# A list scheduler with new costs, a model of VectorE and GpSimd on SBUF, and a new table of priorities

## The chip, the cores and the metric

The kernel runs on one core of one Trainium2 chip. The metric is the device time of one execution in microseconds (us). The kernel before took 1358.99 us (median of three runs, 1357.96 to 1361.76).

In the text PE is the matmul engine (TensorE), DVE is VectorE, ACT is ScalarE, POOL is GpSimd and SP is the engine that issues most transfers.

## The reference, cut to what matters

```
attention, 8 batches x 8 heads, 576 positions x 64; k and v averaged over groups of 8 positions
    -> softmax(q k' / 8) v          = x, 4608 tokens x 512
dense   h = x @ w_in (512 x 2048);  g = h * sigmoid(h);  x = g @ w_out
experts skip = x @ w_skip > 0;  logits = x @ w_gate (8 experts)
    every token with skip > 0 goes to its best expert e:
    x += gate * (relu(x @ w1[e]) @ w2[e])
```

All is float32. Each dense product is split into a high and a low part, so that three matmuls in a faster format (fp32r) replace one.

## The kernel before, in words

There are two stages. The **dense stage** (`dense`, L450) does attention, the dense layer and the routing. Tokens are cut into 36 tiles of 128 and 18 chunks of two tiles (numbers 0 to 17). The **expert stage** (`experts`, L1028) follows in fixed order; its first products (`xm1p`, L952) need the weights of the first expert, split into high and low parts, and gathered tokens.

The dense stage is not written in order. `op(...)` enters each step with its costs per engine, the steps it comes after and the buffers it takes; `schedule` (L649) then issues them one at a time. Among the steps that could start earliest it takes the one with the largest `height`: the length of the longest chain behind it, into which a `bonus` per kind and phase is added (`bonus_of`, L452). Where a step may run on several engines, the one with the lowest end time plus `EXTRA` is taken. Engines then run their own lists strictly in order, each step waiting for its semaphores. The steps that matter below, with their lines:

- `w` (L153) loads 512 KB of a weight; there are 32 such pieces. `abs` L162, `low` L166, `hi` L180 on ACT, `mix` L170 and `or` L175 on DVE turn it into a high part; `lo` (L184, DVE or POOL) makes the low part.
- `vsum` (L221) and `kput` (L201, L205, L207) average v and k. `sc` L260, `mx` L265, `ex` L274, `ns` L279, `nr` L285, `pt` L290, `pc` L231 and `pv` L302 are the attention of one tile; `xh` and `xl` (L318) split its result.
- For each chunk j and each of 16 blocks f: `mm1` (12 matmuls, L324 to L326), `th` L331 on ACT, `sw` L337 on DVE, `gh` L341 on ACT, `gl` (L346, DVE or POOL), `mm2` (6 matmuls, L356 to L358). `mm1` of block f needs the pieces 2f, `mm2` the pieces 2f+1.
- `ev` L365 takes a finished tile out, `st` L371 stores it, 18 `dot` per chunk (L376) give its logits, `ra` (L389 to L397), `rp` (PE, L404), `re` (ACT, L409), `rg`, `rb` (L429 to L437) and `rs` (POOL, L440, two per chunk) place its tokens in the lists of the experts.
- At the end of the dense stage: `ft` (L789 to L805) finds the largest expert from the lists of the chunks up to 15, `fi` (L874) reads its first indices, `l1` and `l2` (L889) load its weights, `ga` (L923) gathers tokens, `xp` (L934) and `xq`/`xr` turn them, `s1h` (L905), `s1l` (L909) split w1, `s2h`, `s2l` split w2. `ft` comes after `rb` of chunk 15, `fi` after `rs` of chunk 15, `l2` and `ti` (L808) after `ra` of chunk 16.

Of the kernel before, what the change touches and what calls it, by code (L numbers as in the profile page):

```python
# [18 lines left out]
B, H, S, D = 8, 8, 576, 64  # L19
# [33 lines left out]
def body(tc, const, q, k, v, w_in, w_out, w_skip, w_gate, w_r, w1, w2, out, x2d, lst, base, nch, nxt):  # L53
# [3 lines left out]
    with ExitStack() as ctx:  # L57
# [94 lines left out]
        def load_w(h):  # L152
            nc.sync.dma_start(out=stage(h), in_=(w_out if h % 2 else w_in)[h // 2])  # L153
# [296 lines left out]
        def dense():  # L450
            ops, last, st = {}, {}, {}
            bonus_of = {  # L452
# [8 lines left out]
            }  # L461
# [13 lines left out]
            def op(name, cost, fn, after=(), take=None, bonus=0.0, linger=0.0):  # L475
                linger += 0.9 * ("S" in cost)
                bonus += bonus_of.get(name[0], {}).get(phase(*name), 0.0)
                ops[name] = (cost, fn, [a for a in after if a], take, bonus, linger)
# [4 lines left out]
            for h in range(2 * NF):  # L483
                op(("w", h), {"S": 1.46}, lambda e, h=h: load_w(h), [h > 3 and ("or", h - 4)])
                last["cx", h] = [("hi", h), ("lo", h)]
                op(("abs", h), {"A": 0.52}, lambda e, h=h: conv_abs(h), [("w", h), h > 0 and ("abs", h - 1)],
                   ("x2", ("cx", h)))
                op(("low", h), {"A": 0.61}, lambda e, h=h: conv_low(h), [("w", h)])
                op(("mix", h), {"V": 0.6}, lambda e, h=h: conv_mix(h), [("abs", h), ("low", h)])
                op(("or", h), {"V": 0.6}, lambda e, h=h: conv_or(h), [("mix", h)])  # L490
                op(("hi", h), {"A": 0.52}, lambda e, h=h: conv_hi(h), [("or", h)])
                op(("lo", h), {"G": 1.23, "V": 0.6}, lambda e, h=h: conv_lo(e, h), [("hi", h)],
                   bonus=-35.6 * h)
# [5 lines left out]
            ways = {0: ["T", "V", "V", "G"], 1: ["VG", "G", "VG", "V"]}  # L499
            price = {"V": 1.34, "G": 2.01}  # L500
            for b in range((tiles * 128 - 1) // S + 1):
                old = b > 1 and ((b - 1) * S - 1) // 128
                for hp in range(HP):
                    s = spot.get(("k", hp)) if b == 0 else None
                    free = [b == 1 and ("clear",), b > 1 and ("sc", old, hp // 2)]
                    last["k", b, hp] = [("kput", b, hp)]
                    op(("k", b, hp), {"S": 0.82}, lambda e, b=b, hp=hp, s=s: put_in((b, hp), k_load(b, hp, s)),
                       [b > 0 and (("k", b, hp - 1) if hp else ("v", b - 1, POOL - 1))], None if s else ("kv", ("k", b, hp)))
# [33 lines left out]
            for i in range(tiles):  # L542
# [3 lines left out]
                last["q", i] = [("sc", i, 1)]  # L546
                op(("q", i), {"S": 0.73}, lambda e, i=i: load_q(i), [i > 0 and ("q", i - 1)], ("q", ("q", i)))
                for g in range(2):
# [23 lines left out]
            for j in range(nch):  # L572
                for f in range(NF):
                    n = slot.get((j, f), -1)

                    def back(name, k):
                        return n - k in at and (name, *at[n - k])

                    last["h", j, f], last["t", j, f], last["g", j, f] = [("sw", j, f)], [("gl", j, f)], [("mm2", j, f)]
                    op(("mm1", j, f), {"T": 1.31}, lambda e, j=j, f=f: put_in(("h", j, f), mm1(j, f)),  # L580
                       [("xl", TPC * j + t) for t in range(TPC)]
# [8 lines left out]
                       [("gh", j, f)], ("gl", ("g", j, f)))  # L590
                    op(("mm2", j, f), {"T": 1.29}, lambda e, j=j, f=f: mm2(j, f),
                       [("gl", j, f), ("lo", 2 * f + 1), f > 0 and ("mm2", j, f - 1), back("mm1", -1)]
# [3 lines left out]
                for t in range(TPC):  # L596
                    i = TPC * j + t
                    dots = [("dot", i, c) for c in range(E + 1)] if j < nch - 1 else []
                    last["x2", i] = dots + [("st", j, t)]
                    op(("ev", j, t), {"A": 0.48, "V": 0.6}, lambda e, j=j, t=t: evac(e, j, t),  # L600
                       [("mm2", j, NF - 1), t > 0 and ("ev", j, t - 1), j > 1 and ("rs", j - 2, TPC - 1), ("or", 2 * NF - 1)],
                       ("x2", ("x2", i)))
                    op(("st", j, t), {"S": 1.46}, lambda e, i=i: store(i), [("ev", j, t)])
                    for c in range(E + 1):
                        if j < nch - 1:
                            op(("dot", i, c), {"V": 0.72}, lambda e, i=i, c=c: dot(i, c), [("ev", j, t), ("router",)])
# [12 lines left out]
            op(("setup",), {"G": 1.5}, lambda e: setup2(), [("lo", 3)])  # L619
            op(("blank",), {"S": 1.0}, lambda e: blank_lists(), [("setup",)])  # L620
            op(("router",), {"S": 8.0}, lambda e: load_router(), [("or", h) for h in range(2 * NF - 4, 2 * NF)])
            ops[("ra", 0)][2].append(("setup",))

            if nxt:
                z, free = nch - 1, ("xl", tiles - 1)
                op(("ft",), {"V": 1.6}, lambda e: first_table(), [free, ("rb", z - 2)])
                ops[("rp", z - 1)][2].append(("ft",))
                op(("fi",), {"S": 0.3}, lambda e: first_idx(), [("ft",)] + [("rs", z - 2, t) for t in range(TPC)])
                op(("l1",), {"S": 6.0}, lambda e: load_1(), [("fi",)])
                op(("l2",), {"S": 6.0}, lambda e: load_2(), [("ra", z - 1), ("l1",)])  # L630
                op(("ga",), {"G": 2.1}, lambda e: gather(0), [("fi",)] + [("st", j, t) for j in range(z) for t in range(TPC)],
# [17 lines left out]
        def schedule(ops, last):  # L649
            unit = {"T": nc.tensor, "A": nc.scalar, "V": nc.vector, "G": nc.gpsimd, "S": nc.sync}  # L650
            room_for = dict(a=2, h=2, o=2 * TPC, x2=4, t=2, gh=3, gl=3, tr=2, kv=3, q=2)
            EXTRA = {"V": 2.34, "G": 0.0, "A": 1.5}
            SIGNAL, SAME, ISSUE, COLD = 0.135, 0.13, 1.75, 30.0

            def gap(a, b):
                if a == b:
                    return SAME * (a != "T")
                return {"T": 0.46, "S": ISSUE}.get(b, SIGNAL + 0.06 * ("T" in a + b or "G" in a + b))

# [13 lines left out]

            held, end, free = {r: [] for r in room_for}, {}, {u: ISSUE * (u == "S") for u in unit}
            known = {}

            def earliest(n):
                if n not in known:
                    known[n] = {}
                    for u in ops[n][0]:  # L680
                        known[n][u] = max([end[d][0] + gap(end[d][1], u)
                                           + ops[d][5] for d in ops[n][2]], default=0.0)
                cost, _, _, take, _, _ = ops[n]
                wait = []
# [539 lines left out]
```

## Time and profile before

| | us |
|---|---|
| median of three runs | 1358.99 |
| the profiled execution | 1359.34 |
| its span, first to last instruction | 1357.6 |
| PE busy | 1279.5 (94%) |
| DVE busy | 817.3 (60%) |
| POOL busy | 642.3 (47%) |
| ACT busy | 567.3 (42%) |

Matmuls are pipelined, so the busy time of PE is no measure of its best speed. The granted TensorE clock has two levels, 1.2 and 2.4 GHz; a window with 0.91 was partly at the lower one. The engine shares are means over stages: the weight pieces are converted in the first 136 us, the dense stage ends at 1005 us, and the expert stage takes the rest.

### The profile page before, as it was taken

How to read it: one execution, taken by the hardware profiler on the slowest of the kernel's cores; microseconds unless marked ns; L12 is line 12 of the kernel's file. 1: busy time of each engine (PE TensorE's matmuls, PEld its weight loads, DVE VectorE, ACT ScalarE, POOL GpSimd, SP SyncE). 2: the span in 40 equal slices, each digit the busy share in tenths (PEclk: the TensorE clock that was granted, in tenths of full speed). 3: DMA queues.
4: the chain of work that ended last, by engine and by line, in shares of the span. 5: the costliest groups of instructions: out<-in, count | busy, mean ns of one | idle time of the engine just before them, and what ended most of it. 6: DMA issues, size and time to landing. Idle time of an engine off the chain costs nothing. (4 is left out here: it accounts for less than half of the span.)

```text
span 1357.6 us, 24535 instructions
## 1 busy us (share of the span) xinstructions
PE 1279.5 (94%) x8508; PEld 1133.2 (83%) x8508; DVE 817.3 (60%) x1963; ACT 567.3 (42%) x1619; POOL 642.3 (47%) x692
## 2 busy tenths in 40 slices
PE   5778999999999999999999999999899999999895
PEld 3557989898888888889888988988789999989674
DVE  7898295276374584574674673759954232333785
ACT  5767443444444334444444443434332121223573
POOL 6889445543653554265366333333652212133664
PEclk9989999999999999999999999999999999999998
DMA  8554131111121121012011110110401111427761
GB/s 244 182 190 169 69 107 31 56 48 40 57 66 43 30 87 48 9 62 79 25 61 41 37 40 12 45 63 1 171 32 48 56 41 56 164 72 257 237 240 36
DMA packets 51311, 113.84 MB, mean 84 GB/s; under 512 B 12311, under 2 KB 13335, under 8 KB 51024
## 3 DMA queue, kind: packets, MB, share of 16 engines
q1 hardware_dynamic: 44960, 96.39, 21.9%
q0 software_dynamic: 6192, 15.49, 3.5%
q8 instruction: 80, 1.31, 0.4%
q14 instruction: 79, 0.65, 0.2%
HBM read 134.58 MB, written 26.62 MB: 119 GB/s over the span
## 5 line engine op out<-in xcount | busy, mean ns | idle before, releaser
L346 POOL TENSOR_TENSOR gl<-t,gh 128x256 fp32r<-128x256 f32 x287 | 234.8, 820 | 314.2 <-ACT gh L341 224.0
L324 PE MATMUL psh<-xh,w_hi 128*128 128x256 f32 x1152 | 334.3, 290 | 12.2 <-DVE t L337 9.8
L326 PE MATMUL psh<-xh,w_lo 128*128 128x256 f32 x1152 | 324.8, 282 | 5.7 <-POOL w_lo L184 5.7
L325 PE MATMUL psh<-xl,w_hi 128*128 128x256 f32 x1152 | 324.7, 282 | 3.0 <-DVE xl L318 3.0
L376 DVE SCALAR_TENSOR_TENSOR junk<-x,wb 128x512 bf16<-128x512 f32 x306 | 268.8, 878 | 14.7 <-ACT x L365 8.5
L324 PEld LDWEIGHTS psh<-xh,w_hi 128*128 128x128 f32 x1152 | 219.0, 190 | 30.3 <-DVE t L337 13.9
L337 DVE SCALAR_TENSOR_TENSOR t<-t,psh 128x256 f32<-128x256 f32 x288 | 119.1, 415 | 206.5 <-ACT t L331 205.5
L356 PE MATMUL pso<-v_hi,gh 128*128 128x512 f32 x576 | 236.1, 410 | 0.8 <-ACT gh L341 0.8
L358 PE MATMUL pso<-v_hi,gl 128*128 128x512 f32 x576 | 227.2, 394 | 6.7 <-POOL gl L346 6.7
L357 PE MATMUL pso<-v_lo,gh 128*128 128x512 f32 x576 | 227.8, 395 | 0.0
L325 PEld LDWEIGHTS psh<-xl,w_hi 128*128 128x128 f32 x1152 | 219.1, 190 | 10.1 <-DVE xl L318 3.2
L326 PEld LDWEIGHTS psh<-xh,w_lo 128*128 128x128 f32 x1152 | 218.8, 190 | 6.5 <-POOL w_lo L184 6.5
L341 ACT CAST gh<-t 128x256 fp32r<-128x256 f32 x288 | 116.9, 407 | 219.3 <-DVE t L337 204.0
L331 ACT ACTIVATE t<-psh 128x256 f32<-128x256 f32 x288 | 110.5, 384 | 211.2 <-PE psh L326 177.7
L358 PEld LDWEIGHTS pso<-v_hi,gl 128*128 128x128 f32 x576 | 109.0, 189 | 37.3 <-POOL gl L346 11.7
L356 PEld LDWEIGHTS pso<-v_hi,gh 128*128 128x128 f32 x576 | 109.1, 189 | 14.9 <-ACT gh L341 1.0
L357 PEld LDWEIGHTS pso<-v_lo,gh 128*128 128x128 f32 x576 | 109.5, 190 | 12.9
L1005 POOL DMA_INDIRECT out_dram<-own,room x27 | 28.2, 1044 | 173.6 <-DVE own L1003 120.3
L961 ACT ACTIVATE v_hi<-p 128x256 fp32r<-128x256 f32 x88 | 33.5, 383 | 183.4 <-PE p L960 175.2
L274 ACT ACTIVATE room<-pss,mx 128x72 f32<-128x72 f32 x288 | 88.3, 319 | 51.6 <-DVE mx L266 48.7
L962 DVE SCALAR_TENSOR_TENSOR v_hi<-p,v_hi 128x256 fp32r<-128x256 f32 x88 | 37.0, 424 | 114.8 <-ACT v_hi L961 102.6
L958 PE MATMUL p<-xh,w_hi 128*128 128x256 f32 x352 | 101.1, 287 | 0.1
(190 smaller groups left out, 2318.2 us busy)
## 6 DMA issues: line engine op xcount, KB each, us to landing
more<-in_w_dram SPq DMA_DIRECT2D x72, 512.0 KB
room<-in_w_dram SPq DMA_DIRECT2D x40, 512.0 KB
wb<-in_w_dram SPq DMA_DIRECT2D x36, 512.0 KB
room<-in_k_dram SPq DMA_DIRECT2D x32, 288.0 KB
room<-in_q_dram SPq DMA_DIRECT2D x36, 256.0 KB
room<-in_v_dram SPq DMA_DIRECT2D x64, 144.0 KB
out_dram<-x SPq DMA_DIRECT2D x36, 256.0 KB
x2d<-x SPq DMA_DIRECT2D x36, 256.0 KB
```

Source lines behind the costliest of these rows:

```text
L324: nc.tensor.matmul(out=ps, lhsT=w4_hi[:, f, kk], rhs=xh[:, kk], start=(kk == 0), stop=False)
L325: nc.tensor.matmul(out=ps, lhsT=w4_hi[:, f, kk], rhs=xl[:, kk], start=False, stop=False)
L326: nc.tensor.matmul(out=ps, lhsT=w4_lo[:, f, kk], rhs=xh[:, kk], start=False, stop=(kk == KD - 1))
L331: nc.scalar.activation(out=t, in_=ps, func=ACTF.Tanh, scale=0.5)
L337: nc.vector.scalar_tensor_tensor(out=t, in0=t, scalar=1.0, in1=ps, op0=ALU.add, op1=ALU.mult)
L341: nc.scalar.copy(out=gh, in_=t)
L346: eng.tensor_tensor(out=gl, in0=t, in1=gh.bitcast(F32), op=ALU.subtract)
L356: nc.tensor.matmul(out=ps, lhsT=gh[:, ts], rhs=v_hi[:, f], start=(f == 0), stop=False)
L357: nc.tensor.matmul(out=ps, lhsT=gh[:, ts], rhs=v_lo[:, f], start=False, stop=False)
L358: nc.tensor.matmul(out=ps, lhsT=gl[:, ts], rhs=v_hi[:, f], start=False, stop=(f == NF - 1))
L376: nc.vector.scalar_tensor_tensor(out=junk, in0=x2_t[i], scalar=1.0, in1=wb[:, e * DM:e * DM + DM], op0=ALU.mult, op1=ALU.mult, accum_out=l ...
L958: nc.tensor.matmul(out=ps, lhsT=W1h4[:, kk, m], rhs=xh[:, kk], start=(kk == 0), stop=False)
```

## The change: new costs, contention and priorities for the scheduler

No instruction's work changes; the steps are the same 3313. New are their costs (`w` and `st` 1.46 to 1.95, `pv`, `mm1`, `mm2` and others), the terms by which an engine is chosen, and the table `bonus_of`, which now has nearly every kind. Transfers go through one modelled queue. A step of DVE in `SHARED` waits in the model for POOL's recent steps, and a step of POOL for DVE's.

```
-                "rb": {0: 40, 1: 120, 3: -216, 8: 160}, "rs": {0: -30, 1: -30, 2: 15, 3: -2},
+                "rb": {0: 42.4, 1: 166.4, 2: -22.6, 3: -214.7, 8: -125.3},
+                "rs": {0: -23.3, 1: -15.7, 2: 19.8, 3: -9.6},
...
+                "dot": {0: 21.8, 1: 111.7, 2: -15.4, 3: 263.4, 8: -143.5}, "w": {0: -236.8},
...
-                linger += 0.9 * ("S" in cost)
...
-                op(("w", h), {"S": 1.46}, lambda e, h=h: load_w(h), [h > 3 and ("or", h - 4)])
+                op(("w", h), {"S": 1.95}, lambda e, h=h: load_w(h), [h > 3 and ("or", h - 4)])
...
-                op(("l1",), {"S": 6.0}, lambda e: load_1(), [("fi",)])
+                op(("l1",), {"S": 8.0}, lambda e: load_1(), [("fi",)])
...
-            EXTRA = {"V": 2.34, "G": 0.0, "A": 1.5}
-            SIGNAL, SAME, ISSUE, COLD = 0.135, 0.13, 1.75, 30.0
+            SHARED, APART = ("ns", "mix", "or", "lo", "nr", "vsum", "vput", "gl", "dot", "kput"), ("rs", "ga", "setup", "ti")
+            FIRST = {"V": 0.786439, "G": 0, "A": 0.394171}
+            LATER = {"V": 1.58663, "G": 0, "A": -0.769199}
+            FILL, HOLD, KEEP = 181.563, 0.9, 0.6
+            SIGNAL, SAME, ISSUE, REACH, COLD, IDLE, WARM = 0.135, 0.05, 0.45, 2.0, 1.8, 3.4, 4.0
...
-                    t = max(free[u], known[n][u])
+                    t, more = max(free[u], known[n][u]), 0.0
...
-                    if u == "T" and t < COLD:
-                        c = 2 * c
-                    rank = t + c + (EXTRA[u] if len(cost) > 1 else 0.0)
-                    if best is None or rank < best[0]:
-                        best = (rank, t, t + c, u)
+                    if u == "S":
+                        return t, t, max(queue[0], t + REACH) + c, u
+                    if u == "T" and (t - quiet[0] > IDLE or ran[0] < WARM):
+                        c = COLD * c
+                    elif u == "V" and n[0] in SHARED:
+                        for a, b in wide["G"][-4:]:
+                            if a <= t + 0.05 and b > t:
+                                t = max(t, a + (b - a) * HOLD)
+                    elif u == "G":
+                        for a, b in wide["V"][-4:]:
+                            if a <= t < b:
+                                t = b
+                        if len(cost) > 1 and t < FILL:
+                            more = KEEP * c
+                    if len(cost) > 1:
+                        more += (LATER if t > FILL else FIRST).get(u, 0.0)
+                    if best is None or t + c + more < best[0]:
+                        best = (t + c + more, t, t + c, u)
...
+                elif u == "G" and n[0] not in APART or u == "V" and n[0] in SHARED:
+                    wide[u].append((t, t1))
```

By count of instructions DVE now has 30 of the 32 `lo` (3 before), 16 of the 56 `vsum` and `vput` (1 before) and 10 of the 288 `gl` (1 before); POOL has the rest, and all 72 `nr` (69 before). The lines from L491 on stand 18 to 39 lines lower in the new file.

**PE, start of the dense layer.** The first `mm1` of chunk 1 (its input is `xh_484` before, `xh_457` after) and what stands ahead of it. Before:

```order
L356 MATMUL pso_496<-v_hi_103,gh_806 128x512
L357 MATMUL pso_496<-v_lo_110,gh_806 128x512
L358 MATMUL pso_496<-v_hi_103,gl_827 128x512
L260 MATMUL pss_865<-room_106 64x144 x4
L324 MATMUL psh_875<-xh_484,w_hi_101 128x256
L325 MATMUL psh_875<-xl_485,w_hi_101 128x256
```

After:

```order
L356 MATMUL pso_491<-v_hi_103,gh_564 128x512
L357 MATMUL pso_491<-v_lo_110,gh_564 128x512
L358 MATMUL pso_491<-v_hi_103,gl_568 128x512
L324 MATMUL psh_596<-xh_457,w_hi_101 128x256
L325 MATMUL psh_596<-xl_458,w_hi_101 128x256
```

Before, ten `mm1` and nine `mm2` of chunk 0 stand ahead of it; after, four of each. From there on the blocks of the two chunks alternate.

**PE, end of the dense stage.** The three last `rp` (L404, L405: `psr`), of chunks 15, 14 and 16. Before, the first two stand among the blocks of chunk 16:

```order
L358 MATMUL pso_10501<-v_hi_103,gl_10962 128x512
L404 LDWEIGHTS triu_94
L404 MATMUL psr_11014<-ohb_10951,triu_94 128x16
L405 LDWEIGHTS ones_95
L405 MATMUL psr_11014<-ohb_10951,ones_95 128x16
L404 LDWEIGHTS triu_94
L404 MATMUL psr_11017<-ohb_10983,triu_94 128x16
L405 LDWEIGHTS ones_95
L405 MATMUL psr_11017<-ohb_10983,ones_95 128x16
L324 MATMUL psh_11022<-xh_10133,w_hi_101 128x256
```

After, all three stand behind the last `mm2` of chunk 17 (`pso_11140`), and the expert stage's `xp` and first product follow:

```order
L358 MATMUL pso_11140<-v_hi_103,gl_11470 128x512
L404 LDWEIGHTS triu_94
L404 MATMUL psr_11484<-ohb_10825,triu_94 128x16
L405 LDWEIGHTS ones_95
L405 MATMUL psr_11484<-ohb_10825,ones_95 128x16
L404 LDWEIGHTS triu_94
L404 MATMUL psr_11487<-ohb_11023,triu_94 128x16
L405 LDWEIGHTS ones_95
L405 MATMUL psr_11487<-ohb_11023,ones_95 128x16
L404 LDWEIGHTS triu_94
L404 MATMUL psr_11636<-ohb_11614,triu_94 128x16
```

What hangs on `rp` of chunks 14 and 15 (`rb`, `ft`, `fi`, `l1`, `ga`) has moved behind the last matmul of the stage with it.

**ACT, end of the dense stage.** The splits of the first expert's w1 (`s1h`: `w_hi<-room`, L905 before, L944 after). Before:

```order
L341 CAST gh<-t 128x256
L905 CAST w_hi<-room 128x1024
L331 ACTIVATE t<-psh 128x256
L905 CAST w_hi<-room 128x1024
L341 CAST gh<-t 128x256
L905 CAST w_hi<-room 128x1024
L331 ACTIVATE t<-psh 128x256
L409 ACTIVATE lg<-lg 128x2x8
L905 CAST w_hi<-room 128x1024
L341 CAST gh<-t 128x256
```

After, behind the last `gh`:

```order
L341 CAST gh<-t 128x256
L365 ACTIVATE x_11537<-pso 128x512
L365 ACTIVATE x_11539<-pso 128x512
L365 ACTIVATE x_11561<-pso 128x512
L365 ACTIVATE x_11570<-pso 128x512
L409 ACTIVATE lg<-lg 128x2x8
L944 CAST w_hi<-room 128x1024 x4
L979 CAST xh<-pst 128x4x128 x2
L944 CAST w_hi<-wb 128x1024 x3
```

The splits stood between the blocks of chunk 17; now they stand behind `re` of chunk 16 (L409), which waits for the 18 `dot` of that chunk. On DVE these 18 `dot` follow `ft`, which follows the last `sw`; on SP `l1` follows the stores of chunk 17.

## Rows read from the trace of the kernel before

**Rows 1.** Windows: engine busy us (instructions), granted clock, DMA share, GB/s.
```profile
core 0: us, PE busy (x) PEld busy (x) DVE busy (x) ACT busy (x) POOL busy (x), PEclk, DMA share, GB/s
40.00:140.00 100.00, 79.22 (x463) 66.66 (x462) 85.44 (x98) 66.14 (x157) 86.18 (x85) 0.91 0.54 180
140.00:180.00 40.00, 40.00 (x308) 35.79 (x306) 17.45 (x41) 20.51 (x67) 20.94 (x23) 1.00 0.24 72
180.00:955.00 775.00, 768.31 (x5363) 684.66 (x5360) 481.33 (x1447) 322.43 (x1075) 357.45 (x442) 1.00 0.14 45
955.00:1006.00 51.00, 46.89 (x286) 41.26 (x285) 39.03 (x89) 20.41 (x43) 32.59 (x29) 0.97 0.33 114
```
**Rows 2.** Timeline of PE: first matmuls of chunks 0 and 1 (start, us, instruction).
```profile
41.36 0.59 PE L324 MATMUL psh<-xh,w_hi 128*128 128x256 f32 x1
...
96.09 0.39 PE L324 MATMUL psh<-xh,w_hi 128*128 128x256 f32 x1
```
**Rows 3.** Lines, 0 to 135 us: count, busy us, mean ns, idle ahead.
```profile
L170 DVE SCALAR_TENSOR_TENSOR cx<-cx,wb 128x512 int32<-128x512 int32 x32 | 41.8, 1307 | 5.6 <-ACT wb L166 3.3 <-POOL room L205 1.3 <-issue 1.0
L175 DVE SCALAR_TENSOR_TENSOR cx<-wb,cx 128x512 int32<-128x512 int32 x32 | 38.0, 1189 | 0.6
...
L184 POOL TENSOR_TENSOR w_lo<-cx,w_hi 128x512 fp32r<-128x512 f32 x15 | 23.8, 1587 | 4.7 <-ACT w_hi L180 4.4
L184 POOL TENSOR_TENSOR v_lo<-cx,v_hi 128x512 fp32r<-128x512 f32 x14 | 22.0, 1571 | 1.5 <-ACT v_hi L180 1.4
L221 POOL TENSOR_TENSOR room<-room 72x512 f32<-72x512 f32 x13 | 19.2, 1480 | 5.7 <-DMA room<-in_v_dram 5.7
```
**Rows 4.** Timeline of DVE, 38 to 53 us.
```profile
38.46 0.66 DVE L184 TENSOR_TENSOR w_lo<-cx,w_hi 128x512 fp32r<-128x512 f32 x1
...
47.35 3.73 DVE L170 SCALAR_TENSOR_TENSOR cx<-cx,wb 128x512 int32<-128x512 int32 x1
...
52.48 0.68 DVE L175 SCALAR_TENSOR_TENSOR cx<-wb,cx 128x512 int32<-128x512 int32 x1
```
**Rows 5.** Timeline of POOL in the same stretch, and its last conversion.
```profile
48.54 0.74 POOL L346 TENSOR_TENSOR gl<-t,gh 128x256 fp32r<-128x256 f32 x1
49.24 1.30 POOL L184 TENSOR_TENSOR w_lo<-cx,w_hi 128x512 fp32r<-128x512 f32 x1
...
134.49 1.30 POOL L184 TENSOR_TENSOR v_lo<-cx,v_hi 128x512 fp32r<-128x512 f32 x1
```
**Rows 6.** Waits of PE, 960 to 1060 us: us in total, times, longest.
```profile
PE psh L324 <- DVE t L337: 4.1, 2, 2.1
```
**Rows 7.** Timeline of DVE, 945 to 968 us.
```profile
945.51 0.16 DVE L389 TENSOR_REDUCE rmx<-lg 128x2 f32<-128x16 f32 x1
...
946.82 0.17 DVE L397 CAST ohb<-oh 128x16 bf16<-128x16 f32 x1
...
949.55 0.16 DVE L429 TENSOR_TENSOR ds<-psr,base 128x8 f32<-128x8 f32 x1
...
950.91 0.16 DVE L437 TENSOR_TENSOR du<-dd,cm 128x2 int32<-128x2 f32 x1
...
954.09 0.15 DVE L794 SCALAR_TENSOR_TENSOR room<-base,room 1x8 f32<-1x8 f32 x1
...
955.90 0.15 DVE L805 TENSOR_TENSOR room<-room 1x8 f32<-1x8 f32 x1
...
967.04 0.69 DVE L376 SCALAR_TENSOR_TENSOR junk<-x,wb 128x512 bf16<-128x512 f32 x1
...
967.76 0.69 DVE L376 SCALAR_TENSOR_TENSOR junk<-x,wb 128x512 bf16<-128x512 f32 x1
```
**Rows 8.** Timeline of POOL, 992 to 1021 us.
```profile
992.90 2.40 POOL L909 TENSOR_TENSOR w_lo<-wb,w_hi 128x1024 fp32r<-128x1024 f32 x1 [0.20 <-ACT w_hi L905]
...
1017.70 1.00 POOL L440 DMA_INDIRECT lst<-row,du  x1 [3.09 <-DVE du L437]
1020.11 0.97 POOL L440 DMA_INDIRECT lst<-row,du  x1 [1.41 <-DMA lst<-row,du]
```
**Rows 9.** Timeline of SP's issues, 964 to 968 us.
```profile
964.81 0.41 SPq L874 DMA_DIRECT2D room<-lst  x1
965.42 2.10 SPq L889 DMA_DIRECT2D room<-in_w_dram  x4
```
**Rows 10.** Timeline of ACT, 993 us: two splits in a row.
```profile
993.45 1.99 ACT L905 CAST w_hi<-wb 128x1024 fp32r<-128x1024 f32 x2
```
**Rows 11.** Timeline of PE, 1015 to 1017 us.
```profile
1015.89 0.28 PE L958 MATMUL p<-xh,w_hi 128*128 128x256 f32 x1
1016.01 0.29 PE L959 MATMUL p<-xl,w_hi 128*128 128x256 f32 x1
...
1016.31 0.41 PE L958 MATMUL p<-xh,w_hi 128*128 128x256 f32 x1
1016.52 0.41 PE L959 MATMUL p<-xl,w_hi 128*128 128x256 f32 x1
```

More of the change, by code (lines that the diff above doesn't have):

```diff
@@ L499, in dense @@
             ways = {0: ["T", "V", "V", "G"], 1: ["VG", "G", "VG", "V"]}
-            price = {"V": 1.34, "G": 2.01}
+            price = {"V": 1.34, "G": 2.4}
             for b in range((tiles * 128 - 1) // S + 1):
@@ L506, in dense @@
                     last["k", b, hp] = [("kput", b, hp)]
[L507 removed]
+                    op(("k", b, hp), {"S": 1.1}, lambda e, b=b, hp=hp, s=s: put_in((b, hp), k_load(b, hp, s)),
                        [b > 0 and (("k", b, hp - 1) if hp else ("v", b - 1, POOL - 1))], None if s else ("kv", ("k", b, hp)))
@@ L546, in dense @@
                 last["q", i] = [("sc", i, 1)]
-                op(("q", i), {"S": 0.73}, lambda e, i=i: load_q(i), [i > 0 and ("q", i - 1)], ("q", ("q", i)))
+                op(("q", i), {"S": 0.98}, lambda e, i=i: load_q(i), [i > 0 and ("q", i - 1)], ("q", ("q", i)))
                 for g in range(2):
@@ L562, in dense @@
                 last["pv", i] = [("xl", i)]
-                op(("pv", i), {"T": 0.8 + 0.24 * len(bs)}, lambda e, i=i, p=pool_f, t=tag: pv_all(i, p, t),
+                op(("pv", i), {"T": 0.95 + 0.35 * len(bs)}, lambda e, i=i, p=pool_f, t=tag: pv_all(i, p, t),
                    [("pc", i, 1), j > 1 and ("mm1", j - 2, NF - 1)]
@@ L579, in dense @@
                     last["h", j, f], last["t", j, f], last["g", j, f] = [("sw", j, f)], [("gl", j, f)], [("mm2", j, f)]
-                    op(("mm1", j, f), {"T": 1.31}, lambda e, j=j, f=f: put_in(("h", j, f), mm1(j, f)),
+                    op(("mm1", j, f), {"T": 1.42}, lambda e, j=j, f=f: put_in(("h", j, f), mm1(j, f)),
                        [("xl", TPC * j + t) for t in range(TPC)]
@@ L590, in dense @@
                        [("gh", j, f)], ("gl", ("g", j, f)))
-                    op(("mm2", j, f), {"T": 1.29}, lambda e, j=j, f=f: mm2(j, f),
+                    op(("mm2", j, f), {"T": 1.39}, lambda e, j=j, f=f: mm2(j, f),
                        [("gl", j, f), ("lo", 2 * f + 1), f > 0 and ("mm2", j, f - 1), back("mm1", -1)]
@@ L602, in dense @@
                        ("x2", ("x2", i)))
-                    op(("st", j, t), {"S": 1.46}, lambda e, i=i: store(i), [("ev", j, t)])
+                    op(("st", j, t), {"S": 1.95}, lambda e, i=i: store(i), [("ev", j, t)])
                     for c in range(E + 1):
@@ L619, in dense @@
             op(("setup",), {"G": 1.5}, lambda e: setup2(), [("lo", 3)])
-            op(("blank",), {"S": 1.0}, lambda e: blank_lists(), [("setup",)])
-            op(("router",), {"S": 8.0}, lambda e: load_router(), [("or", h) for h in range(2 * NF - 4, 2 * NF)])
+            op(("blank",), {"S": 1.15}, lambda e: blank_lists(), [("setup",)])
+            op(("router",), {"S": 9.2}, lambda e: load_router(), [("or", h) for h in range(2 * NF - 4, 2 * NF)])
             ops[("ra", 0)][2].append(("setup",))
@@ L627, in dense @@
                 ops[("rp", z - 1)][2].append(("ft",))
-                op(("fi",), {"S": 0.3}, lambda e: first_idx(), [("ft",)] + [("rs", z - 2, t) for t in range(TPC)])
-                op(("l1",), {"S": 6.0}, lambda e: load_1(), [("fi",)])
-                op(("l2",), {"S": 6.0}, lambda e: load_2(), [("ra", z - 1), ("l1",)])
+                op(("fi",), {"S": 0.2}, lambda e: first_idx(), [("ft",)] + [("rs", z - 2, t) for t in range(TPC)])
+                op(("l1",), {"S": 8.0}, lambda e: load_1(), [("fi",)])
+                op(("l2",), {"S": 8.0}, lambda e: load_2(), [("ra", z - 1), ("l1",)])
                 op(("ga",), {"G": 2.1}, lambda e: gather(0), [("fi",)] + [("st", j, t) for j in range(z) for t in range(TPC)],
@@ L657, in gap @@
                     return SAME * (a != "T")
-                return {"T": 0.46, "S": ISSUE}.get(b, SIGNAL + 0.06 * ("T" in a + b or "G" in a + b))
+                return {"T": 0.43, "S": 0.2}.get(b, SIGNAL + 0.06 * ("T" in a + b or "G" in a + b))
             users, left = {n: [] for n in ops}, {n: len(o[2]) for n, o in ops.items()}
@@ L672, in schedule @@
                 height[n] = min(ops[n][0].values()) + ops[n][4] + max((SIGNAL + height[u] for u in users[n]), default=0)
-            held, end, free = {r: [] for r in room_for}, {}, {u: ISSUE * (u == "S") for u in unit}
-            known = {}
+            held, end, free = {r: [] for r in room_for}, {}, {u: 0.0 for u in unit}
+            known, wide = {}, {"V": [], "G": []}
+            queue, ran, quiet = [0.0], [0.0], [-9.0]
             def earliest(n):
+                cost, _, deps, take, _, _ = ops[n]
                 if n not in known:
[L679 to L683, printed above, removed]
+                    known[n] = {u: max([end[d][0] + gap(end[d][1], u) + ops[d][5] for d in deps], default=0.0)
+                                for u in cost}
                 wait = []
@@ L706, in schedule @@
                 t0 = min(e[1] for e, _ in can)
-                (_, _, t1, u), n = max((c for c in can if c[0][1] <= t0), key=lambda c: height[c[1]])
+                (_, t, t1, u), n = max((c for c in can if c[0][1] <= t0), key=lambda c: height[c[1]])
                 take = ops[n][3]
@@ L712, in schedule @@
                 end[n], free[u] = (t1, u), t1
+                if u == "T":
+                    ran[0], quiet[0] = t1 - t if t - quiet[0] > IDLE else ran[0] + t1 - t, t1
+                elif u == "S":
+                    queue[0], free[u] = t1, t + ISSUE
+                elif u == "G" and n[0] not in APART or u == "V" and n[0] in SHARED:
+                    wide[u].append((t, t1))
                 ready.remove(n)
```

2 lines of the change are left out of this document (1 added, 1 removed), and 31 rows, old and new, of the table bonus_of.

## The prediction, made before the changed kernel ran

> **What bounds the kernel now.** I read the page's shares first (the table above), then the windows by stage, then for each window with idle PE the timelines of the engines that PE waits for. PE is busy for 94% of the span, so only its idle time and its time at the lower clock can be won. [rows 1] show where that lies. From 40 to 140 us PE is busy for 79.22 of 100 us and the granted clock is 0.91; from 140 to 180 it is never idle; from 180 to 955 it is idle for 6.7 us of 775; from 955 to 1006 for 4.1 of 51, at 0.97. So there are two places to look at: the fill, in which the weights are converted, and the end of the dense stage. Between them nothing is to be had and little should be lost.
>
> In the fill the idle time is 100 - 79.22 = 20.8 us. A mean of 0.91 over two levels, of which the lower is half, means that the clock was low for 18% of the window, 18 us; PE did work for some 79% of that, at half speed, so about 7 us are lost to the clock. Together about 28 us. At the end of the dense stage it is 4.1 us and, by the same reckoning (6% of 51 us, halved), 1.5.
>
> Why is PE idle in the fill? In that window DVE is busy for 85.4% and POOL for 86.2% [rows 1]; a block of a chunk can only start when two more pieces are converted. [rows 5] show the last conversion at 134.49. Chunk 1, whose input needs two more tiles of attention, starts at 96.09, 55 us after chunk 0 at 41.36 [rows 2]. Until then each pair of pieces releases one block for PE only: 12 matmuls of 256 columns at 0.12 us [rows 11] and 6 of 512, for which I take twice that: 1.4 + 1.4 = 2.8 us.
>
> **Term 1: the fill.** The change puts chunk 1 behind four blocks of chunk 0 in place of ten (the first of the orders above) and then alternates. From the fifth block on each pair of pieces releases 5.6 us of work, and conversions arrive every 95 / 16 = 5.9 us (41 to 136 us): PE is then nearly full and its clock should stay up. What is not won is the stretch before the fifth block: about 5 us of the 28 lie in its first 16 to 20 us. Of the remaining 23 I leave 3 for the difference of 5.6 and 5.9 and for ACT (66% busy). **20 us are won.** The bounds: 8, if conversions end some 12 us later than they do now, since the blocks that are last in both chunks wait for the last pieces; 33, if the whole 28 goes and chunk 0 also starts 5 us earlier.
>
> Do the conversions keep their pace? DVE takes 27 more `lo`, 0.66 us each when alone [rows 4], 18 us, and 15 averaging sums, for which the nearest row is the same one and POOL's 1.48 [rows 3] the other end: 10 to 22 us, I take 12. POOL loses 27 x 1.58 = 43 us and 15 x 1.48 = 22 us [rows 3]. DVE may get time back too: its `mix` and `or` last 1.307 and 1.189 us on the mean [rows 3], where a single one without company takes 0.68 [rows 4]; 32 x (1.307 + 1.189 - 2 x 0.68) = 36 us of stretching. So DVE's gain of 36 pays for its new 30, and the conversions should end where they do, near 136 us.
>
> The stretch is no rounding: one `mix` started at 47.35 and took 3.73 us, while POOL ran a `gl` of 0.74 at 48.54 and a `lo` of 1.30 at 49.24 [rows 4, 5]. The Trainium skill, page "SBUF — State Buffer", section "Who interferes with whom", states that a DVE instruction with two inputs in SBUF and a POOL instruction that reads SBUF shut each other out for a whole instruction. The row agrees: the `mix` ended about when POOL's two were over. By that rule the two engines' sum counts for the conversions (an estimate: 45 us of DVE and 84 of POOL before, 84 and 48 after, for the kinds that meet), and it stays the same: they would not end sooner, the fill would win by the order of PE alone, and the third rival below would have little to stand on. By the row alone DVE could gain up to the 36 us and end sooner.
>
> **Term 2: the end of the dense stage.** Here the orders show a loss. `rp` of chunks 14 and 15 stood between blocks of chunk 16; now they stand behind the last `mm2` of chunk 17. What depends on them ran under the matmuls of chunks 16 and 17 (`rb` of chunk 15 or 14 at 949.55, `ft` at 954.09, `fi` at 964.81, `l1` at 965.42 [rows 7, 9]); after the change nothing of PE is left to hide it. Let t = 0 be the end of that last `mm2`. The chain in the new order:
>
> - `rp` 15 and 14 and their signals, estimated at 0.6 us. Two `rb`, 949.55 to 951.07 = 1.52 us each [rows 7]: 3.6.
> - `ft`, 954.09 to 956.05 = 1.96 [rows 7]: 5.6. It stands ahead of 18 `dot` of chunk 16 on DVE, 0.72 apart [rows 7]: 18.6. `ra` of chunk 16, 945.51 to 946.99 = 1.48 [rows 7]: 20.0; `re` on ACT, some 0.3: 20.3.
> - ACT has its `s1h` behind that `re`: four at 1.0 [rows 10]: 24.3. In the meantime DVE does `rg` and `rb` of chunk 16 (1.5 and 1.5: 23.5), and POOL has its `rs` ahead of its two `s1l`: 1.0 [rows 8], 24.5.
> - `s1l` on POOL, 2.40 each [rows 8]: 26.9 and 29.3; DVE has two of these in between (twice 0.66 for twice the width [rows 4]), and one of them in POOL's way makes it 30.5.
> - The expert stage's first product needs all quarters of w1, so PE stands until about 30.5 but for its transposes, and then starts at the lower clock: 0.21 us a matmul in place of 0.12 [rows 11], 1.5 us in the first sixteen.
>
> Beside it runs the load: two `rs` per chunk for 14 and 15, 2.41 apart [rows 8], 3.6 + 4 x 2.41 = 13.2 without overlap; `fi`, then `st` of chunk 17, then four issues of `l1` in 2.10 [rows 9]: issued at about 15.5, landed by some 22 us. That is 1 to 2 us earlier than the splits can use it, and so costs nothing; it would be next if the `dot` were quicker.
>
> So PE waits about 30.5 us and loses 1.5 to the clock: 32. What goes is the wait of before: 4.1 us of PE for DVE's `t` [rows 6], in which the `dot` were in the way, and the 1.5 of clock: 5.6. On POOL the splits of w2 (three at 2.40) come into the routing of chunk 17, for which I neither add nor subtract. **About 26 us are lost.** Bounds: 18, if the first quarters' matmuls run while the others are still split and `rb` and `ft` overlap; 36, if the load of w1 lands after the routing and each split comes behind it.
>
> **Term 3: the middle.** From 180 to 955 us PE has 6.7 us of idle time [rows 1], and the new table changes the order of every kind. Nothing there can win more than 6.7; I take 0, with -5 and +4 as bounds, the upper one of the size of the waits of [rows 6]. The queue of transfers exists in the model only; its cost in the kernel is 0, as DMA is at 14% there and at 54% in the fill [rows 1].
>
> **Sum.** The profiled execution took 1359.34 (span 1357.6 and 1.7 around it), 0.35 above the median. 1359.3 - 20 + 26 + 0 = 1365.3, less 0.35: **1365**. With both large terms moving by their middle bounds this forecast's own range is 1361 to 1372.
>
> **Rivals.**
>
> - *The fill wins little.* DVE becomes the engine that everything waits for: if its `mix` and `or` keep half their stretch, it has 18 us more work in a stretch of 95 in which it was busy for 85%, the conversions end 12 us later, and the last blocks of two chunks queue behind them. The fill wins 8 to 10. For it: DVE's 85.4%. Against it: POOL's 65 us less. 1359 - 9 + 26 = 1376. Chance 0.17.
> - *The two cancel.* The end costs only 18 to 22, because the first product runs quarter by quarter and waits for the last split alone. For it: matmuls of the first product are issued by quarters. Against it: the third quarter is among the late ones. 1359 - 20 + 20 = 1359. Chance 0.23.
> - *Faster.* DVE and POOL no longer meet, so conversions end well before 136 us and attention of the first tiles too; chunk 0 starts 5 us sooner and the whole 28 us go. For it: the 36 us of stretching. Against it: the sum of both engines' work. 1359 - 33 + 26 = 1352. It decides as soon as the fill wins 4 us more than the end costs, that is 30. Chance 0.26.
> - *The forecast*, 0.34.
>
> A run of this kernel can tell about 0.3%, 4.1 us, from no change: 1354.9 to 1363.1 is the same. The forecast's lower edge and the first rival are slower, the second is the same and part of the forecast's lower edge is too: faster 0.26, same 0.24, slower 0.50. The range that leaves 2 in 10 outside goes from 1349 to 1379.
>
> **What the new profile would show.** The first `mm1` of chunk 1 near 60 us and not at 96; `mix` and `or` near 0.7 to 0.9 us on the mean; most `lo` on DVE; PE busy for over 90% from 60 to 140 us. At the end a gap of some 30 us of PE between the last `mm2` (L358) and the first product of the expert stage, with a lower granted clock behind it, and the chain of waits going through `dot` (L376), `ra`, `re`, and the splits of w1. It would be wrong in term 1 if the last conversion ended after 145 us or before 125, in term 2 if PE's gap were under 18 us or if the chain went through `l1` and not through the `dot`, in term 3 if the middle changed by over 5 us.

## The result and the profile after

The changed kernel takes 1347.8 us (median of four runs, 1345.03 to 1348.03) against 1358.9 (now four runs): a ratio of 0.991, 95% interval 0.9891 to 0.993. The forecast was 1365, slower, with a range from 1349 to 1379. The sign was wrong, and the time lies below the range. The profiled execution has a span of 1346.3 us, 11.3 less than before.

The windows of [rows 1] in the changed kernel:

```profile
40.00:140.00 100.00, 96.61 (x679) 86.74 (x679) 88.41 (x152) 74.51 (x199) 58.49 (x60) 0.98 0.50 168
140.00:180.00 40.00, 39.75 (x279) 35.40 (x276) 31.74 (x84) 19.53 (x67) 18.92 (x23) 1.00 0.45 154
180.00:955.00 775.00, 774.24 (x5398) 692.60 (x5397) 450.00 (x1374) 323.43 (x1056) 350.07 (x434) 1.00 0.14 43
955.00:1006.00 51.00, 20.97 (x115) 18.31 (x115) 38.07 (x125) 14.18 (x23) 27.74 (x21) 0.65 0.37 135
```

PE's idle time in the fill has gone from 20.8 to 3.4 us and in the middle from 6.7 to 0.8, while the window of the old end now holds a hole: 30 us idle, at a granted clock of 0.65.

The span is best cut at three matmuls of fixed meaning: the last `mm2` (L358) of chunk 2, of chunk 15 and of chunk 17, found by their place in PE's order. Before, then after (start, us, instruction; PE):

```profile
231.56 0.39 PE L358 MATMUL pso<-v_hi,gl 128*128 128x512 f32 x1
...
903.18 0.39 PE L358 MATMUL pso<-v_hi,gl 128*128 128x512 f32 x1
...
1004.87 0.39 PE L358 MATMUL pso<-v_hi,gl 128*128 128x512 f32 x1
```
```profile
204.74 0.39 PE L358 MATMUL pso<-v_hi,gl 128*128 128x512 f32 x1
...
866.47 0.39 PE L358 MATMUL pso<-v_hi,gl 128*128 128x512 f32 x1
...
960.39 0.39 PE L358 MATMUL pso<-v_hi,gl 128*128 128x512 f32 x1
```

| leg, us | before | after | change | forecast |
|---|---|---|---|---|
| fill, to the end of chunk 2 | 231.6 | 204.7 | -26.8 | -20 |
| middle, to the end of chunk 15 | 671.6 | 661.7 | -9.9 | 0 |
| late, to the end of chunk 17 | 101.7 | 93.9 | -7.8 | -5.6 |
| rest, to the end of the span | 352.7 | 385.9 | +33.2 | +32 |
| sum | 1357.6 | 1346.3 | -11.3 | +6.4 |

The last two legs together lose 25.4 us, as forecast (26.4); the gains ahead of them had been put too low, by 6.8 us in the fill and 9.9 in the middle.

**The end.** PE in the changed kernel, behind that last `mm2`:

```profile
960.39 0.39 PE L358 MATMUL pso<-v_hi,gl 128*128 128x512 f32 x1
...
980.01 0.19 PE L404 MATMUL psr<-ohb,triu 128*128 128x16 bf16 x1 [19.14 <-DVE ohb L397]
...
985.23 2.31 PE L973 MATMUL pst<-ident,room 128*128 128x128 f32 x8 [5.00 <-DMA room<-x2d,room]
989.37 0.58 PE L997 MATMUL p<-xh,w_hi 128*128 128x256 f32 x1 [1.83 <-ACT xh L979]
991.87 0.58 PE L998 MATMUL p<-xl,w_hi 128*128 128x256 f32 x1 [1.92 <-DVE xl L983]
...
992.46 0.41 PE L997 MATMUL p<-xh,w_hi 128*128 128x256 f32 x1
992.68 0.41 PE L998 MATMUL p<-xl,w_hi 128*128 128x256 f32 x1
...
997.78 0.28 PE L999 MATMUL p<-xh,w_lo 128*128 128x256 f32 x1
997.90 0.28 PE L997 MATMUL p<-xh,w_hi 128*128 128x256 f32 x1
```

The last column in brackets is PE's wait and its releaser. With t = 0 at 960.6, `rp` of chunk 16 runs at 19.4 (forecast: `ra` at 20.0), the first product at 28.8 (forecast 30.5), and the spacing is 0.12 us again only from 997.8 on, at 37. The same stretch on DVE (the start of `ft`, then the first and last `dot`), SP (`fi`, then `l1`) and ACT (`re`, the four splits of w1, then `xh`, the first token tiles for the product):

```profile
963.95 0.15 DVE L833 SCALAR_TENSOR_TENSOR room<-base,room 1x8 f32<-1x8 f32 x1
...
965.28 0.67 DVE L376 SCALAR_TENSOR_TENSOR junk<-x,wb 128x512 bf16<-128x512 f32 x1
...
977.84 0.69 DVE L376 SCALAR_TENSOR_TENSOR junk<-x,wb 128x512 bf16<-128x512 f32 x1
```
```profile
973.36 0.41 SPq L913 DMA_DIRECT2D room<-lst  x1
...
975.99 2.52 SPq L928 DMA_DIRECT2D room<-in_w_dram  x4
```
```profile
979.08 0.22 ACT L409 ACTIVATE lg<-lg 128x16 f32<-128x16 f32 x1 [17.67 <-DVE oh L391]
982.31 1.04 ACT L944 CAST w_hi<-room 128x1024 fp32r<-128x1024 f32 x1 [3.02 <-DMA room<-in_w_dram]
983.54 1.04 ACT L944 CAST w_hi<-room 128x1024 fp32r<-128x1024 f32 x1 [0.19 <-DMA room<-in_w_dram]
985.74 1.04 ACT L944 CAST w_hi<-room 128x1024 fp32r<-128x1024 f32 x1 [1.15 <-DMA room<-in_w_dram]
987.30 1.04 ACT L944 CAST w_hi<-room 128x1024 fp32r<-128x1024 f32 x1 [0.52 <-DMA room<-in_w_dram]
988.26 1.06 ACT L979 CAST xh<-pst 128x512 fp32r<-128x512 f32 x2
```

The 18 `dot` lie between 965.3 and 978.5, as reckoned from [rows 7]. `l1` is issued at t = 15.4 (forecast 15.5), but its first quarter is used only at 21.7, 3 us behind `re`, and each of the four splits waits for its own quarter, the last until t = 26.7. I had put the landing at some 22, 1 to 2 us ahead of the splits. Behind the splits ACT makes `xh`, which releases the first product. The gathered tokens come no sooner: PE's transposes wait for them until 985.23. So what held PE in the end is the chain through `rp`, `rb`, `rs`, `fi` and then the two transfers `l1` and `ga`; the one through `dot`, `ra` and `re` was done 3 us before it.

**The fill.** First `mm1` of chunks 0 and 1 on PE; DVE's conversions up to 140 us; DVE's last `lo`:

```profile
38.37 0.59 PE L324 MATMUL psh<-xh,w_hi 128*128 128x256 f32 x1
...
55.57 0.28 PE L324 MATMUL psh<-xh,w_hi 128*128 128x256 f32 x1
```
```profile
L175 DVE SCALAR_TENSOR_TENSOR cx<-wb,cx 128x512 int32<-128x512 int32 x32 | 24.9, 789 | 0.0
L170 DVE SCALAR_TENSOR_TENSOR cx<-cx,wb 128x512 int32<-128x512 int32 x32 | 24.0, 764 | 0.9 <-ACT cx L162 0.6 <-ACT wb L166 0.2
```
```profile
137.69 0.69 DVE L184 TENSOR_TENSOR v_lo<-cx,v_hi 128x512 fp32r<-128x512 f32 x1
```

Chunk 1 starts at 55.6 in place of 96.1 [rows 2]; `mix` and `or` fell from 1307 and 1189 ns [rows 3] to 764 and 789. The conversions end at 138.4, hardly later than the 135.8 of [rows 5], which looks as if placement (the engine that a step is given to) had done nothing. The experiments show that it had done much.

### The profile page after: what moved, and what is told of

Its sections match the earlier page's. It is cut to its first block, busy times and chain, and to the rows that moved or that the text cites. A ratio compares the mean times of both kernels' runs of the same rounds, so it can differ in the third digit from the quotient of the medians.

```text
span 1346.3 us, 24483 instructions
## 1 busy us (share of the span) xinstructions
PE 1270.8 (94%) x8508; PEld 1132.8 (84%) x8508; DVE 792.9 (59%) x2011; ACT 568.6 (42%) x1619; POOL 580.4 (43%) x644
## 5 line engine op out<-in xcount | busy, mean ns | idle before, releaser
L346 POOL TENSOR_TENSOR gl<-t,gh 128x256 fp32r<-128x256 f32 x278 | 224.8, 809 | 351.9 <-ACT gh L341 247.8
L376 DVE SCALAR_TENSOR_TENSOR junk<-x,wb 128x512 bf16<-128x512 f32 x306 | 254.7, 832 | 14.8 <-ACT x L365 9.3
L356 PE MATMUL pso<-v_hi,gh 128*128 128x512 f32 x576 | 232.7, 404 | 0.0
L358 PE MATMUL pso<-v_hi,gl 128*128 128x512 f32 x576 | 225.1, 391 | 2.0 <-POOL gl L346 2.0
L325 PEld LDWEIGHTS psh<-xl,w_hi 128*128 128x128 f32 x1152 | 217.7, 189 | 7.1
L341 ACT CAST gh<-t 128x256 fp32r<-128x256 f32 x288 | 117.0, 407 | 161.5 <-DVE t L337 140.1
L358 PEld LDWEIGHTS pso<-v_hi,gl 128*128 128x128 f32 x576 | 108.2, 188 | 28.1 <-POOL gl L346 2.5
L285 POOL TENSOR_TENSOR room<-room,sm 128x288 f32<-128x288 f32 x72 | 61.2, 850 | 101.9 <-DVE sm L280 65.9
```

The lines of the kernel that those rows point to most:

```text
L325: nc.tensor.matmul(out=ps, lhsT=w4_hi[:, f, kk], rhs=xl[:, kk], start=False, stop=False)
L341: nc.scalar.copy(out=gh, in_=t)
L346: eng.tensor_tensor(out=gl, in0=t, in1=gh.bitcast(F32), op=ALU.subtract)
L356: nc.tensor.matmul(out=ps, lhsT=gh[:, ts], rhs=v_hi[:, f], start=(f == 0), stop=False)
L358: nc.tensor.matmul(out=ps, lhsT=gl[:, ts], rhs=v_hi[:, f], start=False, stop=(f == NF - 1))
L376: nc.vector.scalar_tensor_tensor(out=junk, in0=x2_t[i], scalar=1.0, in1=wb[:, e * DM:e * DM + DM], op0=ALU.mult, op1=ALU.mult, accum_out=l ...
```

## The experiments

The four legs of each profiled run, cut at the same three matmuls, and the median of its timed runs. The ratio is to runs of the kernel before on the same chip, whose medians are 1358.3 to 1360.9:

| run | fill | middle | late | rest | median | ratio to before (95%) |
|---|---|---|---|---|---|---|
| before | 231.6 | 671.6 | 101.7 | 352.7 | 1358.9 | |
| after | 204.7 | 661.7 | 93.9 | 385.9 | 1347.8 | 0.991 (0.989 to 0.993) |
| e1_tail | 204.4 | 661.3 | 103.6 | 358.1 | 1329.0 | 0.979 (0.976 to 0.981) |
| e2_pool | 217.7 | 661.8 | 93.9 | 385.3 | 1361.6 | 1.002 (1.001 to 1.004) |
| e3_dve | 217.4 | 671.7 | 101.7 | 352.4 | 1344.7 | 0.990 (0.989 to 0.992) |
| e4_oldtable | 210.6 | 661.9 | 94.4 | 385.9 | 1355.7 | 0.998 (0.997 to 0.999) |
| e5_lo | 223.3 | 671.6 | 101.7 | 353.2 | 1349.8 | 0.991 (0.989 to 0.994) |
| e6_nowide | 217.7 | 680.7 | 97.6 | 382.9 | 1381.8 | 1.016 (1.013 to 1.018) |
| e7_tail2 | 203.8 | 661.2 | 105.2 | 357.0 | 1328.0 | 0.976 (0.973 to 0.978) |
| e8_newtable | 228.8 | 680.9 | 95.1 | 386.3 | 1395.0 | 1.025 (1.023 to 1.028) |
| e9_rp16 | 204.5 | 661.3 | 104.4 | 358.3 | 1330.5 | 0.979 (0.977 to 0.982) |
| e10_dots | 204.3 | 661.3 | 104.4 | 357.6 | 1327.1 | 0.975 (0.973 to 0.977) |

**e1_tail.**
```
-                   [("ra", j)], ("a", ("rp", j)))
+                   [("ra", j)], ("a", ("rp", j)), bonus=600.0 * (j > nch - 5))
```


> The changed kernel with one bonus: rp of chunks 14 to 16 gets 600, so that these small matmuls stand among the blocks of chunk 17 and not behind its last mm2. Theory (the 33 us between the last mm2 and the full speed of the expert stage hang on rp alone): PE goes from the last mm2 to the expert stage without a gap of over 5 us, and the time is 1316 to 1322 us. Rival (the loads of w1 and the gathered tokens and the splits are late in any case, since VectorE and GpSimd are apart in the model only): 10 to 18 us of the gap stay, 1330 to 1338 us.

Measured: 1329.0. The rest falls by 27.8 us to 358.1, near the 352.7 of before, so the loss of the last leg hangs on `rp`; but the late leg grows by 9.7. Of the 25.4 us that both legs lost, 18.1 come back. Neither expectation was met in its number. PE's waits from 900 to 1010 us say where:

```profile
PE psr L404 <- DVE ohb L397: 9.2, 2, 5.7
PE p L998 <- DVE xl L983: 2.0, 1, 2.0
PE pso L358 <- POOL gl L346: 1.4, 1, 1.4
```

`rp` of chunks 16 (3.5 us) and 17 (5.7) still wait for their `ra`. The bonus moves more than `rp`, since it counts in the height of all that leads to it: on DVE the 18 `dot` of chunk 16 now stand between the ninth and the fifteenth of the 16 `sw` of chunk 17, and not behind the last.

**e2_pool.**
```
+                here = u
+                if n[0] in ("lo", "vput") or n[0] == "vsum" and n[1] < 2:
+                    here = "V" if n in (("lo", 4), ("lo", 27), ("lo", 31), ("vsum", 1, 7)) else "G"
-                ops[n][1](unit[u])
+                ops[n][1](unit[here])
```


> The changed kernel with its order, but lo and the averaging sums of the first two batches on the engines that the kernel before gave them to (29 of 32 lo on GpSimd). Theory A (the fill is won by PE's order, chunk 1 after four blocks): most stays, at most 8 us longer than the changed kernel, 1347 to 1356 us, chunk 1 starts near 56 to 60 us. Theory B (it is won by keeping the two engines apart): mix and or are stretched again to 1.2 us and more, the conversions end past 145 us, and 20 to 30 us are lost: 1368 to 1378 us.

**e3_dve**: the same five lines in the kernel before, with GpSimd for `lo` 1 and 22 and sums 1 and 4 of the second batch, and VectorE for the others.

> The other way round: the kernel before with its order, but lo and those sums on the engines that the changed kernel gives them to (30 of 32 lo on VectorE). Theory A (order): chunk 1 still starts after ten blocks, so PE keeps its idle time in the fill; 1355 to 1363 us. Theory B (placement): conversions come faster, and with them everything on PE; 1332 to 1342 us.

1361.6 and 1344.7 both lie between the ranges of the two theories. With before and after they are the four corners of placement (of `lo` and those sums) and order (all else that the scheduler decides), and neither theory alone holds. In the fill, placement wins 14.2 us with the old order (231.6 to 217.4) and 13.0 with the new one (217.7 to 204.7); the order wins 13.9 and 12.7. They add. `mix` up to 140 us and the last `lo` in e2_pool, then in e3_dve:

```profile
L170 DVE SCALAR_TENSOR_TENSOR cx<-cx,wb 128x512 int32<-128x512 int32 x31 | 37.8, 1237 | 0.7 <-ACT cx L162 0.3 <-ACT wb L166 0.2
```
```profile
150.81 0.68 DVE L184 TENSOR_TENSOR v_lo<-cx,v_hi 128x512 fp32r<-128x512 f32 x1
```
```profile
L170 DVE SCALAR_TENSOR_TENSOR cx<-cx,wb 128x512 int32<-128x512 int32 x32 | 28.5, 892 | 1.8 <-ACT wb L166 1.7
```
```profile
121.34 0.68 DVE L184 TENSOR_TENSOR v_lo<-cx,v_hi 128x512 fp32r<-128x512 f32 x1
```

Placement alone brings the end of the conversions from 135.8 to 122.0; the new order alone puts it off to 151.5; that two chunks then ask for DVE and ACT at once is the likely reason, which no run isolates. Together they give 138.4: two shifts of 13 to 16 us that hide each other. How they make the fill is seen from the end of the last `lo` to the end of the leg: 95.8 us before and 95.4 in e3_dve, 66.2 in e2_pool and 66.4 after. The order sets how much PE has left behind the last piece, some 29 us less in the new one; the placement sets when that piece comes, and at a given order each us of it is a us of the leg.

**e4_oldtable** (the new scheduler with the old `bonus_of`) and **e8_newtable** (the old scheduler with the new one).

> The changed kernel with the old table of bonuses (bonus_of of the kernel before); costs, queue and the model of the two engines are the new ones. Its order has chunk 1 after five mm1 and rp of chunks 14 and 15 behind the last mm2, like the changed kernel. Theory A (the fill hangs on chunk 1 standing early, and the end on rp): 1345 to 1354 us. Rival (the table carries the middle, where 9 us went, and the fill's fine order): 1357 to 1370 us.

> The kernel before with the new table of bonuses alone; costs, the choice of engines and the rest of the scheduler are the old ones. Its order has chunk 1 after ten mm1 as before, lo on GpSimd as before, and rp of chunks 14 and 15 behind the last mm2 as after. Theory (fill by order and placement, end by rp): the loss of the end without a gain, 1380 to 1390 us. Rival (the table carries gains of its own): 1360 to 1375 us.

e4_oldtable: 1355.7, just above the first range. The middle keeps its whole gain (661.9), so it comes from the scheduler's costs and model, which also choose the engines; the table is worth 5.9 us of the fill (210.6 to 204.7). e8_newtable: 1395.0, worse than both expectations: in the old scheduler the new table even loses 9.3 us in the middle. In both, `rp` stands behind the last `mm2`, with a rest of 386 us: either half of the change brings the late order by itself.

**e5_lo**: as e3_dve, with `if n[0] == "lo":` as the condition.

> The kernel before with its order, and only lo on the engines of the changed kernel (30 of 32 on VectorE); the averaging sums stay on GpSimd, unlike in e3_dve. Theory (the 1.58 us of each lo on GpSimd, on the way of every conversion, are what the placement wins): 1344 to 1349 us, as e3_dve. Rival (the sums, 13 of 1.48 us on GpSimd, carry half of it): 1350 to 1355 us.

1349.8, between the two ranges. The fill is 223.3: `lo` alone wins 8.3 us, the averaging sums the other 5.9. The last `lo` ends at 127.6, and again 95.7 us are left.

```profile
126.89 0.68 DVE L184 TENSOR_TENSOR v_lo<-cx,v_hi 128x512 fp32r<-128x512 f32 x1
```

**e6_nowide.**
```
-                        for a, b in wide["G"][-4:]:
-                            if a <= t + 0.05 and b > t:
-                                t = max(t, a + (b - a) * HOLD)
+                        pass
...
-                        for a, b in wide["V"][-4:]:
-                            if a <= t < b:
-                                t = b
```


> The changed kernel without the two loops in which a step of VectorE waits in the model for GpSimd's recent steps and the other way round; the costs, the queue, the terms per engine and the table stay. Theory (keeping the two apart in time wins the 8 us of the middle and some of the fill): 1354 to 1362 us, with the middle slower. Rival (it is the placement that counts, the spacing in time does nothing): 1345 to 1351 us.

1381.8, far above both. The fill is 13.0 us longer than after, the middle 19.0, of which 14.9 are idle time of PE (15.7 against 0.8). PE's waits from 180 to 940 us, then the `dot` of its middle:

```profile
PE psp L290 <- POOL room L285: 11.3, 6, 3.8
PE psh L324 <- DVE t L337: 4.7, 4, 3.2
PE pso L358 <- POOL gl L346: 1.2, 1, 1.2
```
```profile
L376 DVE SCALAR_TENSOR_TENSOR junk<-x,wb 128x512 bf16<-128x512 f32 x233 | 199.2, 855 | 14.8 <-ACT x L365 9.9
```

The changed kernel, then the kernel before, in the same view of waits:

```profile
PE psh L324 <- DVE t L337: 0.6, 1, 0.6
PE psp L290 <- POOL room L285: 0.2, 1, 0.2
```
```profile
PE psh L324 <- DVE t L337: 3.3, 4, 1.3
PE pso L358 <- POOL gl L346: 3.2, 4, 1.0
```

So the loops win much, but not by what their name says: without them the `dot` is no more stretched (855 ns; 860 after, 872 before). They change the modelled times, and by them the order and the engines too: without them DVE gets 25 of the `gl` and 14 of the `nr`, with them 10 and none. What they take away is above all PE's wait for `nr` on POOL (L285). In the fill the last `lo` ends at 117.0 without them, sooner than in any other run, and yet 100.7 us are left behind it: soon converted is of no use if the order leaves PE more to do afterwards. Order and engines were not told apart here, nor why they are so sensitive to the loops.

**e7_tail2, e9_rp16, e10_dots**, on the changed kernel (e7: `rp` of chunks from 14 on at 720, `dot` at -80; e9: 640, no `dot`; e10: these lines):
```
+                if name[0] == "rp" and 13 < name[1] < 16:
+                    bonus += 720.0
+                elif name[0] == "dot" and name[1] > 29:
+                    bonus += -80.0
```


> As e1_tail, with rp of chunks 14 to 17 at 720 and the dots of tiles 30 and later at 80 less, so that rp of chunks 14 and 15 stand some blocks earlier. Theory (what is left of the gap in e1_tail, 9.2 us of PE waiting for ohb and 2.0 for xl, comes from the routing starting 10 us late): 1320 to 1326 us. Rival (those waits belong to chunk 17's own routing and stay): 1327 to 1331 us.

> As e1_tail, with 640 for rp of chunks 14 and 15 only; rp of chunk 16 now stands two places before the last mm2 and no longer five, behind the first transposes xp. Theory (PE's 3.5 us at rp of chunk 16 and the low clock that follows it are a matter of place): 1321 to 1326 us. Rival (what PE would wait for there it waits for one step later, since the splits and the tokens are not ready either): 1327 to 1331 us.

> As e9_rp16, with 720 for rp of chunks 14 and 15 and the dots of tiles 30 and later at 80 less, so that rp of both stand four blocks earlier in the list and the whole routing of chunk 16 with them. Theory (the earlier the routing, the less of the end is left): 1318 to 1325 us. Rival (the end is set by what comes behind the last mm2): the same as e9_rp16 within 2 us.

1328.0, 1330.5 and 1327.1: the same as e1_tail within their intervals. For e7_tail2 and e9_rp16 that is what the rivals had. e10_dots lies 3.3 us under e9_rp16, neither in the theory's range nor within the rival's 2 us, and its edit did less than was expected of it: `rp` of chunks 14 and 15 moved ahead by one block, not by four (43.5 us ahead of the last `mm2` of chunk 17 in place of 40.7). e9_rp16 shows that `rp` of chunks 14 and 15 are enough: the rest is 358.3 with these two alone raised, though there too the `dot` of chunk 16 moved with them. Its waits, 900 to 1010 us:

```profile
PE psl L1064 <- DVE x2T L1059: 6.3, 1, 6.3
PE psr L404 <- DVE ohb L397: 4.5, 1, 4.5
```

The wait for `ohb` of chunk 17 (5.7 us in e1_tail) is gone, and another one for DVE takes its place; that of chunk 16 stays, 4.5 us now. All four beat both kernels: the one before by 2.1 to 2.5%, the changed one, by the quotient of the ratios, by 1.2 to 1.6%.

## Why the prediction was wrong

In spans the forecast was +6.4 us and the result -11.3. Of the 17.7 us between them 9.9 lie in term 3, 6.8 in term 1 and 1.0 in term 2. Without the miss of term 3 the time would have stood near 1358, inside the range.

- **Term 3, the middle: the step that failed most** is "Nothing there can win more than 6.7; I take 0". It put at nothing a stage that then won 9.9 us. The waits of 3.3 us for `sw` on DVE and 3.2 for `gl` on POOL went almost wholly, and PE's idle time in the leg fell from 6.0 to 0.8 (0.1 in e4_oldtable). By the two orders one `mm1` and one `mm2` less lie in the leg, and one `sc` more: an estimate of 2.4 us, from the prediction's 2.8 us for a block. Some 2 us stay open; the bars of neighbouring matmuls overlap by 0.16 us (0.28 long, 0.12 apart [rows 11]) and could hide short waits, which is not shown. e4_oldtable shows that the scheduler's costs and model bring the gain without the table, and e6_nowide that it is lost without the two loops.
- **Term 1, the fill: the step that failed** is "DVE's gain of 36 pays for its new 30, and the conversions should end where they do". They do end there (138.4 for 136), but by luck, as the sum of two shifts. The step left out that POOL loses 65 us of the same chain while DVE still has 6 to spare, so that at a given order the conversions come 13 to 14 us sooner; and that the new order puts them off by 16 stood in a bound alone. All 20 us were booked to PE's order. At a given placement the order wins 12.7 to 13.9, at a given order the placement 13.0 to 14.2, together 26.8.
- The sentence on the Trainium skill's page "SBUF — State Buffer", section "Who interferes with whom", erred in the same place. The rule itself agrees with the traces: `mix` goes from 1307 to 892 ns when only placement changes. But the estimate by it put the sum of both engines at 132 us after the change (84 + 48), whereas the prediction's own terms give DVE 45 + 30 and POOL 84 - 65, 94 in all. A `lo` takes 1.30 us on POOL [rows 5] and 0.66 on DVE [rows 4], so a move makes the sum shorter. Rightly added, the sum says that conversions come sooner at a given order, as they did in e3_dve.
- **Term 2, the end: right in size, wrong in its path, and so in part luck.** -5.6 and +32 against -7.8 and +33.2. The cause is as forecast: every run with `rp` behind has a rest of 383 to 386 us, every run with it ahead 352 to 358. But the splits waited for `l1` and not for `dot`, `ra` and `re`, which the prediction had named as a sign that the term is wrong. The "landed by some 22 us" came from no row; the last quarter was used at 26.7. In the sum PE's first product waits for the low parts too; it started behind the four high parts, at 28.8 and not at 30.5. What PE lost behind it, at the lower clock and in a wait of 1.9 for `xl`, was more than the 1.5 reckoned. These errors cancel. Whether the `dot` would set the end if the transfers came sooner was not run.
- **The rivals.** "Faster" gave 1352 by a fill of 33 us: its sign was right and its mechanism half so, as the conversions did come sooner by placement, but the order took that back. The 3 us by which chunk 0 starts earlier (38.4 against 41.4) were in it too. "The fill wins little" is refuted by the 26.8 us: DVE is busier than before (88.4 of 100 us) and the conversions still end at 138.4. Its "18 us more work" was a slip; 30 less half of 36 is the 12 that it went on with.

## What to carry to other kernels

When work moves from one engine to another, price its chain and not the two engines' balance: an end of a phase that stays where it was can be two shifts that cancel, and only one change at a time shows them. Do not put a stage at nothing because its engine is 99% busy: its idle time went almost wholly here, and some 2 us more that are unexplained. What ends a phase is two things, when the last input comes and how much is left to do behind it; measure both. A list scheduler puts a tiny step with a long tail of other engines behind all the large ones if its height says so; look for such steps at the end of a stage, and raise them by name: one line took 19 us off the span here (1346.3 to 1327.4).

## What was not expected of the hardware

Behind the hole PE ran at half speed for some 8 us after its first product: from 989.4 to 997.8 the granted clock was 0.50, the lower of the two levels, and the matmuls stood 0.21 us apart, then 0.12. In the hole ahead of that it was busy for 2.7 of 28.8 us; before the hole, from 900 on, for all of 60.6 us, at 1.00. One `mix` on DVE took 3.73 us where an `or` of the same size took 0.68 [rows 4]. It ended at 51.08, 0.54 us after a `gl` and a `lo` on POOL that ran one behind the other [rows 5], as if it had waited for whole instructions and not been slowed in proportion. The mean of `mix` follows how much POOL has of the conversions and sums, not how many instructions DVE has: 1237 to 1320 ns with 29 or 30 `lo` on POOL (e2_pool, before, e8_newtable), 972 with two and the sums as before (e5_lo), 764 to 892 with two and few sums (after, e1_tail, e3_dve, e4_oldtable).
